# When the mixer tiles run, what lies in the value step, and how the last keys are loaded, in a decode-attention kernel that streams its cache

## The chip, the cores and the metric

The kernel runs on one core of one Trainium2 chip. The metric is the time of one execution in device microseconds. The engines by their names in the profile: PE multiplies matrices (PEld is its weight load), DVE and ACT work on vectors, SP issues the large DMA transfers, POOL does a few instructions at the start. The profile also gives PEclk, the share of its full clock that PE was granted.

## What is computed

One token is decoded: a gated sum of grouped-query attention over a cache of 65,536 positions and a small token-mixing MLP.

```python
Hq, Hkv, Sk, Dh = 16, 8, 65536, 256          # x is 1 x 448
q = (x @ wq), by heads;  k, v: each of the 8 cached heads serves 2 query heads
scores = q @ k.T * Dh**-0.5
a = softmax(scores) @ v, heads side by side, @ wo

h = layernorm(x)
u = gelu(outer(h, w1) + b1)                   # 448 x 1792, tanh form
b = u @ w2 + b2                               # 448

g = sigmoid(sum(x * gate_w))
out = g * a + (1 - g) * b
```

All is bf16. K and V are 268 MB each, so 537 MB of the 544 MB that the kernel reads are cache.

## The kernel before

**Pairs.** For each of the 8 cached heads (H) the 65,536 positions are cut into 4 parts (PPH) of 16,384. A part is called a pair here, a pair of one K load and one V load of 8 MB each; there are NP = 32. A pair's keys are 128 tiles of 128 positions (NV), worked on in 8 chunks (BODY) of 16 tiles. V is held in one buffer of 128 tiles (`vbuf`), K in a ring of one and a half (`kring`, NV + HV tiles, HV = 64): the half of it at HV holds the first four chunks of every pair, and the other four lie in turn at 0 and at NV.

**A pair on PE.** `keys` (L371) transposes chunks 0 to 6 into PSUM (`transposes`, L331, the tile `kst`), and after each but the first multiplies the chunk before by the two queries (`scores`, L356). DVE and ACT bring the transposed banks to SBUF (`evacuate`, L670, into `ktT`, two banks on DVE, two on ACT at L812). Transposing into a bank waits until the chunk before in it was evacuated (L342). `values` (L404) then adds the products of the pair before: 8 matmuls for the denominators (L391), 128 with the V tiles (`some`, L396). `last_keys` (L378) does chunk 7, and `maxima` (L384 on PE, L678 on DVE) finds the running maximum over the partitions. ACT makes the exponentials (`weights`, L793), DVE rescales the accumulator (L695 to L703) and announces it on `s_acc`.

**The loop of PE** (L537 to L580) has NP + LEAD + 1 = 35 passes. Registers say whether a pass does keys (L538), values (L550) or a last chunk (L569); what a pass doesn't do is jumped over. In the first passes values of pair 0 come before keys of pair 1, and so on; from pair 3 on a pass is: keys of pair j, values of pair j - 1, last chunk of pair j, maxima of pair j.

**The code of `values`** holds, in this order: denominators, the first 48 products for the usual pair, the last pair's alternative (four products of the mixer's row with the gate, L419, and 48 products with V tiles that were loaded into `kring`), products 48 to 112, products 112 to 128, and for the last pair the whole tail (`tail`, L475: products by the other operand order, L443, and the last projection, L469). Behind `values`, and ahead of the last chunk, stands the end of a head (L558 to L568): PE clears the accumulator, sums it over the rows (L455) and projects it with wo (L466).

**DVE's loop** (L746 to L762): chunks 0 to 6 evacuated; at the first pair of a new head `finish_head` (L724) for the head before; chunk 7; maxima; in pairs 0 to 13 one tile of the mixer (`mixer`, L643); behind a head's last pair the new queries (`qcur`, L760), which PE's keys wait for (L543). A mixer tile is 11 DVE instructions on 128 x 448 (L649 to L667) and one tanh on ACT (L816); PE multiplies it with w2 one pair later (L574 to L578).

**The order of the loads** (SP, L282 to L306) is written out and waits by semaphores. K of pair j is issued once PE has transposed four chunks of pair j - 1 (L287); V of pair j, once values of pair j - 1 are done (`sem_pv`, L275). For a new head SP then waits for the old head's projection and loads the next wo (L278 to L280). V of the last pair comes in pieces (L301 to L306): 48 tiles into `kring` once pair 30's keys are transposed, the other four pieces once its values are done, then wo in two pieces. All of these go through one queue, in the order of their issue.

K of pair LEAD = 2 and of pair 3 are loaded in halves with semaphores of their own (`sem_kc`, L197, L285 to L292), which PE waits for at chunk 4 (L336 to L338).

Of the kernel before, what the change touches and what calls it, by code (L numbers as in the profile page):

```python
# [7 lines left out]
AF = mybir.ActivationFunctionType  # L8
# [4 lines left out]
def bass_gated_mix__gqa_block_cached__mixer_token_mlp__decode_kernel(  # L13
# [63 lines left out]
    GC0 = 0.796875  # L77
    GC1 = 0.044677734375

    assert FT <= NP - PPH  # L80

# [13 lines left out]
    with ctx:  # L95
# [98 lines left out]

        sem_k = new_sem("sem_k")
        sem_kb = new_sem("sem_kb")
        sem_kc = [new_sem("sem_kc%d" % i) for i in range(2)]  # L197
# [55 lines left out]
        def _(eng):  # L253
# [28 lines left out]
            for j in range(NP):  # L282
                if j == LEAD + 1:
                    eng.wait_ge(sem_tr[NB - 1], BODY * LEAD)
                    load(kring, A_k_cache, j, HV, NV, HV, sem_kc[1])  # L285
                if j >= 1:
                    eng.wait_ge(sem_tr[NB - 1], BODY * (j - 1) + DC)  # L287
                if j == LEAD:
                    load(kring, A_k_cache, j, HV, NV, 0, sem_k)
                    load(kring, A_k_cache, j, 0, HV, 0, sem_kc[0])  # L290
                elif j == LEAD + 1:
                    load(kring, A_k_cache, j, 0, HV, HV, sem_k)  # L292
                elif j >= 1:
# [33 lines left out]
        def _(pe):  # L327
# [3 lines left out]
            def transposes(k, c, j, u16, x2):  # L331
                if k == 0:
                    pe.wait_ge(sem_k, u16)
                if k == DC:
                    pe.wait_ge(sem_kb, 16)
                    for i, sem in enumerate(sem_kc):  # L336
                        with pe.If(j == LEAD + i):
                            pe.wait_ge(sem, 16)  # L338

                def tiles(at):  # L340
                    for b in range(NB):
                        pe.wait_ge(sem_ev[b], c + 1)  # L342
                        for i in range(4):
                            ins = pe.transpose(kst[:, b, i * P:(i + 1) * P],  # L344
                                               kring_f[:, at + NT * (k % DC) + 4 * b + i, :], ident[:, :])
# [56 lines left out]
                return ins  # L402

            def values(v):  # L404
                def last(f):
                    with pe.If(v == NP):
                        f()

                pe.wait_ge(s_acc, v)
                pe.wait_ge(sem_exp, pe.snap(v + 1, min_val=2, max_val=NP + 1))  # L410
                denominators()
                with pe.If(v < NP):
                    pe.wait_ge(sem_v, pe.snap(v * 16, min_val=16, max_val=16 * NP))
                    some(0, NRING, vbuf)
                with pe.Else():
                    pe.wait_ge(s_mix, 1)
                    for q in range(NCG):
                        r = slice(32 * q, 32 * q + 1)
                        pe.matmul(prj[r, 0:WG], rest[r, :], brow[r, :], start=False, stop=True,  # L419
                                  skip_group_check=True)  # L420
                    piece_wait(0)
                    some(0, NRING, kring)
                for n0, n1 in pieces[1:]:
                    if n0 < NLATE:
                        last(lambda: piece_wait(n0))
                        ins = some(n0, n1, vbuf)
                ins.then_inc(s_early, 1)
                with pe.If(v < NP):
                    some(NLATE, NV, vbuf).then_inc(sem_pv, 1)
                with pe.Else():  # L430
                    tail()

            def piece_wait(n):
                for (n0, _), sem in zip(pieces, sem_vp):
# [95 lines left out]
            gk_reg = reg("gk_reg", 1)  # L530
            mv_reg = reg("mv_reg", 0)
            gv_reg = reg("gv_reg", 1)
            def val(r, lo=0, hi=NP):
                return pe.snap(r, min_val=lo, max_val=hi)

            on = OrderedEngineSet([pe.engine])
            with nc.Fori(0, NP + LEAD + 1, 1, engines=on, head_slot={pe.engine: 0}):  # L537
# [12 lines left out]
                with pe.If(val(v_reg) < val(l_reg)):  # L550
# [4 lines left out]
                    values(v)  # L555
                    with pe.If(v >= LEAD):
                        pe.reg_mov(cap_reg, NP)
                    with pe.If(val(mv_reg) == PPH):  # L558
                        with pe.If(v < NP):
                            pe.reg_mov(mv_reg, 0)  # L560
                            g1 = pe.snap(gv_reg, min_val=1, max_val=H)
                            pe.wait_ge(s_cp, g1)
                            clear(acc[:, 0:NACC])
                            by_row(acc[:, SELC:NACC]).then_inc(s_sel, 1)
                            pe.wait_ge(sem_wo, pe.snap(g1 * 16, min_val=16, max_val=16 * H))
                            pe.wait_ge(s_oTn, g1)
                            project(range(2 * REP)).then_inc(s_proj, 1)
                            pe.reg_add(gv_reg, gv_reg, 1)  # L568
                with pe.If(val(l_reg) < val(k_reg)):  # L569
                    l = pe.snap(l_reg, min_val=0, max_val=NP - 1)  # L570
                    last_keys(pe.snap(l * BODY, min_val=0, max_val=NC), pe.snap(x2l_reg, min_val=0, max_val=NV))
                    pe.reg_sub(x2l_reg, NV, x2l_reg)
                    with pe.If(l > 0):
                        with pe.If(l < FT + 1):  # L574
                            pe.wait_ge(s_pb, val(l_reg, 1))
                            for q in range(NCG):
                                pe.matmul(prj[32 * q:32 * q + 1, WG:2 * WG], w2cur[:, :],
                                          gu[:, q * WG:(q + 1) * WG], start=False, stop=True, skip_group_check=True)  # L578
                    pe.reg_add(l_reg, l_reg, 1)
                    maxima(pe.snap(l_reg, min_val=1, max_val=NP))  # L580

        @block.vector
        def _(vec):
# [192 lines left out]
        def _(act):  # L776
# [12 lines left out]

            pt_reg = act.alloc_register("pt_reg")  # L790
            act.reg_mov(pt_reg, DC)

            def weights(j1):  # L793
                act.wait_ge(s_mneg, j1)
# [11 lines left out]
            with nc.Fori(0, NP, 1, engines=OrderedEngineSet([act.engine])) as j:  # L806
# [4 lines left out]
                        act.wait_ge(sem_tr[b], c0 + (k + 1))  # L811
                        act.activation(ktT[:, k % KTB, b, :], kst_b[:, b, :], AF.Copy).then_inc(sem_ev[b], 1)  # L812
                weights(act.snap(j + 1, min_val=1, max_val=NP))
                with act.If(j < FT):
                    act.wait_ge(s_u, j + 1)
                    act.activation(z_b[:, :], z_b[:, :], AF.Tanh).then_inc(s_tanh, 1)  # L816
# [32 lines left out]
```

## Time and profile before

| | us |
|---|---|
| three executions | 1271.89, 1272.1, 1273.35 (median 1272.1) |
| the profiled execution: its own time | 1273.45 |
| its span, first to last instruction | 1271.7 |
| PE busy (matmuls) / weight loads | 941.5 / 884.7 |
| ACT busy / DVE busy | 545.8 / 498.2 |
| DMA: read in all, mean rate | 544.22 MB, 428 GB/s |

The busy times are shares of the whole span (74, 70, 43 and 39%) and say nothing of single stages. The large queue (q1) carried 544.22 MB, and its packets took 99.2% of 16 engines' span. In a timeline a row is: start, duration, engine, line, operation, output <- input, shape, count, and in brackets how long the engine had been idle and what ended that. "issue" there means that the profile shows nothing that the engine waited for. In a windows view a row is: window, its length, then for each engine busy time and count, then granted clock, DMA share and GB/s.

### The profile page before, as it was taken

The numbers are of one execution on the slowest core, as the hardware profiler recorded it, in microseconds if no ns is written. First come the engines' busy times: TensorE is split into PE (matmuls) and PEld (weight loads), VectorE is DVE, ScalarE is ACT, GpSimd is POOL, SyncE is SP. The second block draws the span as 40 slices with busy tenths as digits, with TensorE's granted clock in tenths as the row PEclk, the third lists the DMA queues.
The fourth block names the chain that finished last, engine by engine and source line by source line (L and its number), as shares of the span: only waits on it lengthen the run. The fifth ranks groups of instructions, "written<-read, shape, count | busy, mean of one in ns | idle before, by whom it ended". The sixth has DMA issues, their size and how long they took to land.

```text
span 1271.7 us, 40084 instructions
## 1 busy us (share of the span) xinstructions
PE 941.5 (74%) x17201; PEld 884.7 (70%) x17201; DVE 498.2 (39%) x1125; ACT 545.8 (43%) x692; POOL 0.9 (0%) x7
## 2 busy tenths in 40 slices
PE   4678877787676787766877667786678766698667
PEld 3567767787675786756877567776668766687666
DVE  3335444444543434433434234342333332343333
ACT  2345443454433544434544335453344443344432
POOL 0000000000000000000000000000000000000000
PEclk9889688888878988878977789877798877888778
DMA  9999899999999999999999999999999999999998
GB/s 415 430 399 428 377 429 429 443 429 429 429 429 443 429 429 451 439 410 449 441 429 429 443 429 429 429 443 429 429 429 429 443 429 429 429 451 439 429 429 344
DMA packets 11912, 544.40 MB, mean 428 GB/s; under 512 B 1401, under 2 KB 1660, under 8 KB 2940
## 3 DMA queue, kind: packets, MB, share of 16 engines
q1 hardware_dynamic: 11810, 544.22, 99.2%
q8 instruction: 9, 0.15, 0.0%
q10 hardware_dynamic: 90, 0.01, 0.0%
q14 instruction: 3, 0.02, 0.0%
HBM read 544.22 MB, written 0.00 MB: 428 GB/s over the span
## 4 chain that ended last, share of the span: by engine, by line
DMA 61%; PE 35%; DVE 2%; issue 2%; DVEq 0%; ACT 0%; SPq 0%
DMA kring<-in_A_k_cache_dram 61%; PE kst L344 27%; PE sps L365 6%; PE acc L400 2%; PE sps L388 0%; DVE mcol L680 0%; ACT z_b L816 0%; PE acc L458 0%; PE sps L386 0%; PE acc L393 0%; DVE ktT L674 0%; DVE mrow L685 0%; DVE z_b L655 0%; DVE wtmp L653 0%; DVE z_b L659 0%
## 5 line engine op out<-in xcount | busy, mean ns | idle before, releaser
L344 PE MATMUL kst<-ident,kring 128*128 128x128 f32 x4096 | 574.9, 303 | 251.6 <-DMA kring<-in_A_k_cache_dram 198.0
L812 ACT ACTIVATE ktT<-kst 128x1024 bf16<-128x1024 bf16 x512 | 500.4, 1021 | 560.7 <-PE kst L344 560.0
L344 PEld LDWEIGHTS kst<-ident,kring 128*128 128x128 f32 x4096 | 522.2, 158 | 266.6 <-issue 259.7
L674 DVE COPY ktT<-kst 128x1024 bf16<-128x1024 bf16 x512 | 354.0, 692 | 606.3 <-PE kst L344 582.2
L365 PEld LDWEIGHTS sps<-qcur,ktT 128*128 128x128 bf16 x8192 | 239.4, 97 | 3.0
L365 PE MATMUL sps<-qcur,ktT 128*128 128x2 bf16 x8192 | 237.5, 163 | 0.0
L400 PE MATMUL acc<-vbuf,pT 128*2 128x256 bf16 x4032 | 121.6, 281 | 2.9 <-issue 2.9
L400 PEld LDWEIGHTS acc<-vbuf,pT 128*2 128x2 bf16 x4032 | 94.2, 86 | 21.9 <-issue 3.4
L795 ACT ACTIVATE fade<-mdif 128x2 f32<-128x2 f32 x32 | 6.5, 203 | 93.6 <-DVE mdif L691 93.6
L388 PEld LDWEIGHTS sps<-mdiag,mones 2*128 2x128 f32 x64 | 12.1, 234 | 28.1 <-DVE mdiag L687 28.1
L680 DVE TENSOR_REDUCE mcol<-sps 128x2 f32<-128x256 f32 x32 | 13.6, 425 | 45.7 <-PE sps L365 45.7
L388 PE MATMUL sps<-mdiag,mones 2*128 2x2 f32 x64 | 14.8, 299 | 21.3 <-DVE mdiag L687 21.3
L799 ACT ACTIVATE pT<-sps,mneg 128x64 f32 x128 | 30.3, 334 | 0.0
L816 ACT ACTIVATE z_b<-z_b 128x448 bf16<-128x448 bf16 x14 | 8.1, 576 | 48.1 <-DVE z_b L661 48.1
L386 PE MATMUL sps<-ident,mcol 128*2 128x128 f32 x32 | 9.3, 292 | 18.7 <-DVE mcol L683 18.7
L393 PE MATMUL acc<-pT,ones_sq 128*128 128x32 bf16 x256 | 11.7, 179 | 9.8 <-DVE acc L703 5.2
L708 DVE COPY accs<-acc 128x288 f32<-128x288 f32 x8 | 3.7, 458 | 38.8 <-PE acc L400 38.8
L386 PEld LDWEIGHTS sps<-ident,mcol 128*2 128x2 f32 x32 | 2.6, 80 | 22.1 <-DVE mcol L683 22.1
L393 PEld LDWEIGHTS acc<-pT,ones_sq 128*128 128x128 bf16 x256 | 8.6, 97 | 12.4 <-issue 7.0
L703 DVE TENSOR_SCALAR acc<-acc,fader 128x256 f32<-128x256 f32 x32 | 15.8, 493 | 2.5
L685 DVE TENSOR_REDUCE mrow<-sps 2x1 f32<-2x128 f32 x32 | 8.9, 279 | 12.3 <-PE sps L386 12.3
L690 DVE TENSOR_SCALAR mneg<-sps 128x2 f32<-128x2 f32 x32 | 5.1, 159 | 17.8 <-PE sps L388 17.8
(108 smaller groups left out, 169.4 us busy)
## 6 DMA issues: line engine op xcount, KB each, us to landing
kring<-in_A_k_cache_dram SPq DMA_DIRECT2D x6, 4096.0 KB, 23.6
wo_sb<-in_A_wo_dram SPq DMA_DIRECT2D x7, 448.0 KB, 32.0
vbuf<-in_A_wq_dram SPq DMA_DIRECT2D x1, 3072.0 KB, 10.6
kring<-in_A_v_cache_dram SPq DMA_DIRECT2D x1, 3072.0 KB, 38.3
vbuf<-in_A_v_cache_dram SPq DMA_DIRECT2D x1, 3072.0 KB, 10.1
vbuf<-in_A_v_cache_dram SPq DMA_DIRECT2D x1, 1024.0 KB, 12.2
vbuf<-in_A_v_cache_dram SPq DMA_DIRECT2D x1, 768.0 KB, 13.7
vbuf<-in_A_wq_dram SPq DMA_DIRECT2D x1, 512.0 KB, 11.4
```

What stands on the lines that cost most here:

```text
L344: ins = pe.transpose(kst[:, b, i * P:(i + 1) * P], kring_f[:, at + NT * (k % DC) + 4 * b + i, :], ident[:, :])
L365: ins = pe.matmul(sps[:, 0, 2 * (NT * k + nt):2 * (NT * k + nt) + 2], ktT[:, par, b, ntl * DH + dj:(ntl + 1) * DH:2], qcur[:, dj, :], star ...
L386: pe.transpose(mxT, mcol[:, :], ident[:, :]).then_inc(s_mT, 1)
L388: pe.matmul(mxB, mones[:, :], mdiag[:, :], start=True, stop=True).then_inc(s_mB, 1)
L393: pe.matmul(acc[:, DENC:SELC], ones_sq[:, :], pT[:, r, :], start=False, stop=(r == BODY - 1), skip_group_check=True)
L400: ins = pe.matmul(acc[o:o + REP, 0:DH], pT[:, r, 2 * nt:2 * nt + 2], buf[:, n, :], start=False, stop=False, skip_group_check=True)
L674: vec.tensor_copy(ktT[:, k % KTB, b, :], kst_b[:, b, :]).then_inc(sem_ev[b], 1)
L680: vec.tensor_reduce(out=mcol[:, :], in_=scores_all.rearrange("p (n hh) -> p hh n", hh=REP), axis=AX.X, op=ALU.max)
L685: vec.tensor_reduce(out=mrow[:, :], in_=mxT, axis=AX.X, op=ALU.max)
L703: vec.tensor_scalar(acc[:, 0:DENC], acc[:, 0:DENC], fader[:, :], None, op0=ALU.mult).then_inc(s_acc, 1)
L799: ins = act.activation(pT[:, bass.ds(p0, DC), hh:2 * NT:REP], scores_all.rearrange("p (a r n hh) -> p a hh r n", a=2, r=DC, hh=REP)[:, hal ...
L812: act.activation(ktT[:, k % KTB, b, :], kst_b[:, b, :], AF.Copy).then_inc(sem_ev[b], 1)
```

## The change

Four edits.

1. **Mixer tiles** run in pairs 4 to 17 (MIX0 = LEAD + 2) instead of 0 to 13, on DVE, ACT and PE alike.
2. **The value step** loses its alternatives: `values` now holds the denominators, 128 products and the waits, 136 matmuls with their weight loads. The last pair's first products (mixer's row, 48 products with `kring`) become `first_of_last`, which stands behind `maxima` of the last pair in the loop's body; the tail stands at the end of the loop's body.
3. **The end of a head** moves from behind `values` to behind `last_keys`, ahead of the mixer's product and of `maxima`; on DVE `finish_head` moves behind the evacuation of chunk 7.
4. **K of the last pair** is loaded in two halves of 4 MB, the second with a third semaphore `sem_kc[2]`, which PE waits for at chunk 4.

```diff
+    MIX0 = LEAD + 2
...
+                elif j == NP - 1:
+                    load(kring, A_k_cache, j, 0, HV, HV, sem_k)
+                    load(kring, A_k_cache, j, HV, NV, HV, sem_kc[2])
...
-                    for i, sem in enumerate(sem_kc):
-                        with pe.If(j == LEAD + i):
+                    for p, sem in zip((LEAD, LEAD + 1, NP - 1), sem_kc):
+                        with pe.If(j == p):
                             pe.wait_ge(sem, 16)
...
             def values(v):
...
                 denominators()
                 with pe.If(v < NP):
                     pe.wait_ge(sem_v, pe.snap(v * 16, min_val=16, max_val=16 * NP))
                     some(0, NRING, vbuf)
-                with pe.Else():
-                    pe.wait_ge(s_mix, 1)
-                    for q in range(NCG):
...
-                    piece_wait(0)
-                    some(0, NRING, kring)
                 for n0, n1 in pieces[1:]:
...
                 with pe.If(v < NP):
                     some(NLATE, NV, vbuf).then_inc(sem_pv, 1)
-                with pe.Else():
-                    tail()
+
+            def first_of_last():
+                pe.wait_ge(s_acc, NP)
+                pe.wait_ge(sem_exp, NP + 1)
+                pe.wait_ge(s_mix, 1)
+                for q in range(NCG):
+                    r = slice(32 * q, 32 * q + 1)
+                    pe.matmul(prj[r, 0:WG], rest[r, :], brow[r, :], start=False, stop=True,
+                              skip_group_check=True)
+                piece_wait(0)
+                some(0, NRING, kring)
...
                     values(v)
...
-                    with pe.If(val(mv_reg) == PPH):
-                        with pe.If(v < NP):
-                            pe.reg_mov(mv_reg, 0)
...
                 with pe.If(val(l_reg) < val(k_reg)):
...
                     last_keys(pe.snap(l * BODY, min_val=0, max_val=NC), pe.snap(x2l_reg, min_val=0, max_val=NV))
                     pe.reg_sub(x2l_reg, NV, x2l_reg)
-                    with pe.If(l > 0):
-                        with pe.If(l < FT + 1):
-                            pe.wait_ge(s_pb, val(l_reg, 1))
+                    with pe.If(val(mv_reg) == PPH):
+                        pe.reg_mov(mv_reg, 0)
+                        g1 = pe.snap(gv_reg, min_val=1, max_val=H)
+                        pe.wait_ge(s_cp, g1)
+                        clear(acc[:, 0:NACC])
+                        by_row(acc[:, SELC:NACC]).then_inc(s_sel, 1)
+                        pe.wait_ge(sem_wo, pe.snap(g1 * 16, min_val=16, max_val=16 * H))
+                        pe.wait_ge(s_oTn, g1)
+                        project(range(2 * REP)).then_inc(s_proj, 1)
+                        pe.reg_add(gv_reg, gv_reg, 1)
+                    with pe.If(l > MIX0):
+                        with pe.If(l < MIX0 + FT + 1):
+                            pe.wait_ge(s_pb, val(mix_reg, 1, FT))
+                            pe.reg_add(mix_reg, mix_reg, 1)
...
                     maxima(pe.snap(l_reg, min_val=1, max_val=NP))
+                    with pe.If(val(l_reg) == NP):
+                        first_of_last()
+                with pe.If(val(v_reg) == NP):
+                    tail()
...
-                    for k in range(BODY - 1):
+                    for k in range(BODY):
                         evacuate(k, c0 + k)
                     with vec.If(j > 0):
                         with vec.If(m < 1):
                             finish_head(g)
-                    evacuate(BODY - 1, c0 + (BODY - 1))
                     maxima(vec.snap(j + 1, min_val=1, max_val=NP), c0)
-                    with vec.If(j < FT):
-                        mixer(j)
+                    with vec.If(j >= MIX0):
+                        with vec.If(j < MIX0 + FT):
+                            mixer(vec.snap(kt_reg, min_val=0, max_val=FT - 1))
...
-                with act.If(j < FT):
-                    act.wait_ge(s_u, j + 1)
+                with act.If(j >= MIX0):
+                    with act.If(j < MIX0 + FT):
+                        act.wait_ge(s_u, act.snap(mix_reg, min_val=1, max_val=FT))
```

More of the change, by code (lines that the diff above doesn't have):

```diff
@@ L78, in bass_gated_mix__gqa_block_cached__mixer_token_mlp__decode_kernel @@
     GC1 = 0.044677734375
-    assert FT <= NP - PPH
+    MIX0 = LEAD + 2
+    assert MIX0 + FT <= NP - PPH
     HV = NV // 2
@@ L196, in bass_gated_mix__gqa_block_cached__mixer_token_mlp__decode_kernel @@
         sem_kb = new_sem("sem_kb")
-        sem_kc = [new_sem("sem_kc%d" % i) for i in range(2)]
+        sem_kc = [new_sem("sem_kc%d" % i) for i in range(3)]
         s_qc = new_sem("s_qc")
@@ L404, in values @@
             def values(v):
-                def last(f):
-                    with pe.If(v == NP):
-                        f()
                 pe.wait_ge(s_acc, v)
@@ L414, in values @@
                     some(0, NRING, vbuf)
-                with pe.Else():
-                    pe.wait_ge(s_mix, 1)
-                    for q in range(NCG):
-                        r = slice(32 * q, 32 * q + 1)
-                        pe.matmul(prj[r, 0:WG], rest[r, :], brow[r, :], start=False, stop=True,
-                                  skip_group_check=True)
-                    piece_wait(0)
-                    some(0, NRING, kring)
                 for n0, n1 in pieces[1:]:
                     if n0 < NLATE:
-                        last(lambda: piece_wait(n0))
+                        with pe.If(v == NP):
+                            piece_wait(n0)
                         ins = some(n0, n1, vbuf)
@@ L532, in _ @@
             gv_reg = reg("gv_reg", 1)
+            mix_reg = reg("mix_reg", 1)
             def val(r, lo=0, hi=NP):
@@ L557, in _ @@
                         pe.reg_mov(cap_reg, NP)
-                    with pe.If(val(mv_reg) == PPH):
-                        with pe.If(v < NP):
-                            pe.reg_mov(mv_reg, 0)
[L561 to L568, printed above, removed]
                 with pe.If(val(l_reg) < val(k_reg)):
@@ L791, in _ @@
             act.reg_mov(pt_reg, DC)
+            mix_reg = act.alloc_register("mix_reg")
+            act.reg_mov(mix_reg, 1)
             def weights(j1):
@@ L813, in _ @@
                 weights(act.snap(j + 1, min_val=1, max_val=NP))
-                with act.If(j < FT):
-                    act.wait_ge(s_u, j + 1)
-                    act.activation(z_b[:, :], z_b[:, :], AF.Tanh).then_inc(s_tanh, 1)
+                with act.If(j >= MIX0):
+                    with act.If(j < MIX0 + FT):
+                        act.wait_ge(s_u, act.snap(mix_reg, min_val=1, max_val=FT))
+                        act.activation(z_b[:, :], z_b[:, :], AF.Tanh).then_inc(s_tanh, 1)
+                        act.reg_add(mix_reg, mix_reg, 1)
             act.wait_ge(s_proj, H)
```

## The prediction

> **What bounds the kernel now.** I read the page first, then the table by stage, then the timeline of four places, then the landings of the big loads.
>
> ```profile
> span 1271.7 us, 40084 instructions
> ...
> DMA packets 11912, 544.40 MB, mean 428 GB/s; under 512 B 1401, under 2 KB 1660, under 8 KB 2940
> ```
>
> The transfers fill the span. By the trace's landings a K or V load of 8 MB lands 19.36 us after the one before it (V 429.44, K 448.80, V 468.14), which is the pace of the stream; from K of pair 6 on (253.95) none is more than 0.3 us behind that, wo loads of 1.1 us aside. So time can only come from the places where the stream stops, from before it starts, or from after it ends. There are three. The first is the windows view around 150 us (bytes are booked where a packet starts):
>
> ```profile
> 145.00:150.00 5.00, 5.00 (x75) 4.94 (x72) 1.38 (x2) 2.70 (x3) 0.00 (x0) 0.50 0.97 419
> 150.00:152.00 2.00, 2.00 (x11) 2.00 (x11) 0.69 (x1) 0.32 (x2) 0.00 (x0) 0.50 0.00 0
> 152.00:154.50 2.50, 2.33 (x40) 2.18 (x38) 0.69 (x1) 1.88 (x2) 0.00 (x0) 0.66 0.00 0
> 154.50:157.00 2.50, 2.21 (x33) 2.21 (x34) 1.34 (x2) 1.12 (x3) 0.00 (x0) 1.00 1.26 419
> ```
>
> The last two columns are DMA share and GB/s: for 4.5 us no packet starts, while PE is busy at a granted clock of 0.50. The timeline says what SP was waiting for:
>
> ```profile
> 134.65 3.67 PE L344 MATMUL kst<-ident,kring 128*128 128x128 f32 x16 [0.68 <-issue]
> ...
> 135.74 0.34 DVE L649 TENSOR_SCALAR wtmp<-hbT,params 128x448 bf16<-128x448 bf16 x1 [0.18 <-issue]
> ...
> 139.71 0.39 DVE L667 TENSOR_TENSOR gu<-wtmp,z_b 128x448 bf16<-128x448 bf16 x1
> 140.42 1.29 DVE L674 COPY ktT<-kst 128x1024 bf16<-128x1024 bf16 x2 [0.32 <-issue]
> 141.17 3.67 PE L344 MATMUL kst<-ident,kring 128*128 128x128 f32 x16 [2.85 <-DVE ktT L674]
> ...
> 153.57 0.33 SPq L264 DMA_DIRECT2D kring<-in_A_k_cache_dram  x1
> ```
>
> Pair 3's first chunk is transposed at 134.65, but DVE evacuates it only after pair 2's mixer tile (L649 to L667), so the second chunk waits 2.85 us. Four chunks must be transposed before K of pair 4 is issued, and that is at 153.57; V of pair 2 had landed at 152.09, its last packets started at 149.3. K of pair 4 lands 23.25 us after it: **3.89 us lost** (23.25 - 19.36).
>
> The second place is earlier. V of pair 1 lands at 93.65, K before it at 72.46: 21.19, so **1.83 us lost**. Its issue waits for the first value step:
>
> ```profile
> 51.43 3.54 PE L344 MATMUL kst<-ident,kring 128*128 128x128 f32 x16 [8.06 <-issue]
> ...
> 60.87 4.32 PE L400 MATMUL acc<-vbuf,pT 128*2 128x256 bf16 x80
> ...
> 68.09 2.52 PE L400 MATMUL acc<-vbuf,pT 128*2 128x256 bf16 x48 [2.90 <-issue]
> ...
> 70.64 0.33 SPq L264 DMA_DIRECT2D vbuf<-in_A_v_cache_dram  x1
> 74.70 5.59 PE L344 MATMUL kst<-ident,kring 128*128 128x128 f32 x32 [4.09 <-issue]
> ```
>
> "issue" gaps of 8.06, 2.90 and 4.09 us occur in the first passes only; over the rest of the loop the longest is 0.7 (waits view, 250 to 1215). The page's queue row counts 9 instruction packets on q8, and all 9 start before 78 us (at 43.4, 48.3, 65.6 and 70.4 just inside these gaps). So these are code that PE reaches for the first time: the jump over the value step (8.06, two packets), the step's product 80 (2.90), the jump over the head's end.
>
> The third place is the tail: after V of pair 30 lands (1247.04), PE still has a value step, the last chunk, maxima, exponentials and the last products.
>
> ```profile
> 1248.31 3.66 PE L400 MATMUL acc<-vbuf,pT 128*2 128x256 bf16 x128
> 1252.02 1.86 SPq L264 DMA_DIRECT2D vbuf<-in_A_v_cache_dram  x4
> ...
> 1260.99 2.73 PE L400 MATMUL acc<-kring,pT 128*2 128x256 bf16 x48
> 1263.51 3.35 PE L400 MATMUL acc<-vbuf,pT 128*2 128x256 bf16 x64
> ```
>
> Here stream and PE end together: the last wo piece lands at 1268.60, PE's last late product ends at 1268.86.
>
> **The change, part by part.**
>
> *Mixer in pairs 4 to 17.* Fourteen tiles of 4.4 us (135.74 to 140.10) on DVE are moved, none removed. Pairs 0 and 1 had them hidden: K of pair 1 lands at 72.46, the tile of pair 0 ends at 65.0; pair 1's ends at 106.9, DVE is next needed at 110.36. Pair 2's goes: DVE is free at 135.55, PE runs chunks 0 and 1 back to back, 134.65 to 142 at the half clock. In every later pair where PE ran 32 transposes in one go the clock rose 2.9 to 5.5 us after their start (254.08 to 259.5, 331.69 to 334.59); in pair 3 the split run stayed at half until 153.68. With the clock up by 137.6 to 141, chunk 3 ends at 144.8 to 147 and K is issued then; it takes 0.96 us to its first packet (153.57 to 154.53) and the stream has room until 149. So the whole 3.89 goes, with 1 to 3 us to spare. In pairs 4 to 17 the tile lies beside the wait for K: PE waited 184.9 us in 25 pairs (7.4 each) with tiles in a third of them, and every pair from 253.95 on starts within 0.2 us of its K. Tightest is pair 4, with a head's end: values at about 190, last chunk, head's end, maxima, tile to about 211, K of pair 5 at about 208; K of pair 6 goes out near 220.5, room until 224.4. Cost 0; uncovered, it would be at most what pair 3 shows.
>
> *Value step of 272 instructions.* The jump skips 136 products and their weight loads (272), not 263 (526): the two ring variants, the tail and the head's end lie behind it now. At least one packet of the 8.06 gap should go (about 3.5 us by the 2.9 and 4.09 gaps), and the step is short enough that no code in it is skipped whole before its first run, so the 2.90 should go too. Bounds: 0 gained if packets fall on other boundaries, 1.83 if V of pair 1 is issued before about 68.5. I take 1.8: it needs 2.1 us of some 6. The stream then reaches K of pair 3 1.8 us sooner (118.64, at most 1 us of room); pair 1's keys start at 72.6 in place of 74.70 without the 2.24 us after K's landing, so that issue moves up 2.1 as well.
>
> *Head's end behind the last chunk.* 25 products, DVE's finish and SP's wait before the wo load (up to 2.8 us now, some 4 more then; next on SP is a K load 20 us later). DVE's finish stands behind eight evacuations; queued behind it are the maxima, needed by the next value step 25 us on. Cost 0, covered by the same 7.4 us per pair.
>
> *Last K load in two halves, first products behind the last maximum.* One DMA more (0.4 us of issue, queue full: 0). The first half lands 9.7 us sooner, at 1217.7; PE begins pair 31 at about 1220.6 (maxima end 1219.8) instead of 1227.82, chunk 4 at 1232 finds the second half (1227.7), and keys end at about 1240.5 (20 us as now). But the value step needs V of pair 30, 1247.04, and PE then stands idle for 6 us. It starts 1 us sooner than now (1248.02), but at the half clock: 54 ns a product (4.32/80 above) until one full clock step of 3.41 us was busy, against 28.6 (3.66/128). That is 5.2 to 6.8 us, so it ends at 1252.4 to 1254.0, not 1251.97: **+0.4 to +2.0, I take +1.2**, and the four V issues at 1252.02 move with it, as do last chunk, maxima and exponentials. Then the loop's return (1.6 us in the timeline at 107.97, mostly run ahead of the 2.7 us of products) and the 0.4 us of denominators, which now lie under the wait for the mixer's row, come between the 48 products and the 64: +0.4 to +1.5; a clock already up would give back 1. Together the end comes **1.6 us later** against the stream (from -0.5, if the clock holds, to +2.8).
>
> The Trainium skill, "TensorE: Matmul & The Clock Gate", under "What's actually happening", has the array fall to half after an idle window of about 3.4 us and rise after a busy one. The trace's clock records agree (only 0.5 and 1.0, steps of 3.41 us). By that rule the split load costs the tail; without it the sum would be 1 us better.
>
> Sum: -3.89 - 1.83 + 1.6 = -4.1 us. The profiled execution took 1273.45 (span 1271.7 and 1.75 around it), so 1269.3 after. The runs' median is 1272.1, 1.35 below. If those runs lost less at 150 us (the half clock there ends by a chance of phase), 1269.3 stands; if they are shorter otherwise, 1268.0. I take the middle: **1268.7**, -0.27%.
>
> **Rivals.**
> 1. *The tail costs nothing or gains* (the clock holds through the idle 6 us, or PE's head start carries): -5.7 - 0.5 gives 1267.3 to 1265.9. For it: V's four issues come after a gap of 0.5 us in the stream that could close. Against: every idle stretch of 5 us in the trace shows 0.5. 0.17.
> 2. *A stall comes back*: pair 1's fetches stay, because the step is no shorter for the machine than it was (1.83 not gained), or pair 5 breaks up as pair 3 did, 18.9 us from first transpose to issue, 2.9 us lost. 1268.7 + 1.8 to 2.9 gives 1270.5 to 1271.6. Against: the room worked out above. 0.20.
> 3. *Slower: code at the end is fetched late.* First products and tail run once, behind the loop's body. If their code isn't in PE's store when reached, each jump costs what L550's did, 3.5 to 7.6 us; it decides once both are missed: 1268.7 + 7.6 gives 1276.3. Against: the tail ran for the first time at 1261 to 1269 before, without an issue gap or a q8 packet. 0.05. The Trainium skill, "Runtime: NRT & Kernel Launch", "Instruction fetch mechanics", says that a taken branch out of a two-page window forces a fetch; by that, misses would recur in every pass, and no q8 packet after 78 us bears it out here.
>
> The forecast (1267.3 to 1270.5) has 0.58. A measurement here tells about 0.2%, 2.5 us: faster needs under 1269.6. Forecast mostly (0.48 of 0.58) and rival 1 fall there: 0.65; same 0.29; slower 0.06. The range takes in rival 1's middle and rival 2: 1266.3 to 1272.2.
>
> **What would show it.** Right: no window near 150 without packets, K of pair 4 landing 19.4 after V of pair 2; gaps of 8.06 and 2.90 smaller, V of pair 1 landing 19.4 after K; pair 31's value step at clock 0.50 and longer than 5 us; 48 and 64 products apart. Wrong: a packetless window elsewhere, an issue gap at the end, or the value step of pair 31 at full clock.

## The result, and the profile after

The changed kernel takes 1269.23 us (median of 15 executions, 1267.54 to 1270.73), the kernel before 1273.85 (15 executions beside them, 1269.61 to 1274.74). The ratio is 0.9968 [0.996, 0.9976]: **faster by 0.32%**. The profiled execution of the changed kernel took 1268.60 with a span of 1266.8; the one of before took 1273.45.

The page of the changed kernel:

```profile
span 1266.8 us, 40261 instructions
...
DMA packets 12054, 544.37 MB, mean 430 GB/s; under 512 B 1417, under 2 KB 1676, under 8 KB 2956
...
q8 instruction: 7, 0.11, 0.0%
```

The same bytes at 430 GB/s in place of 428; q8 had 9 packets before.

The windows view of the changed kernel around 150 us (columns: window, length, busy time of PE, PEld, DVE, ACT and POOL with counts, PEclk, DMA share, GB/s):

```profile
143.00:147.00 4.00, 3.33 (x55) 3.24 (x54) 1.87 (x4) 2.44 (x3) 0.00 (x0) 1.00 0.76 328
147.00:149.00 2.00, 2.00 (x45) 1.99 (x44) 0.91 (x2) 1.44 (x2) 0.00 (x0) 1.00 1.22 524
149.00:151.50 2.50, 2.50 (x49) 2.49 (x48) 1.30 (x3) 1.94 (x2) 0.00 (x0) 1.00 0.97 419
151.50:154.00 2.50, 2.35 (x65) 2.19 (x66) 1.12 (x2) 1.94 (x2) 0.00 (x0) 1.00 0.97 419
```

The clock is 1.00 where it was 0.50, and the stretch without packets is gone. The timeline of the changed kernel has the reason:

```profile
132.65 6.05 PE L348 MATMUL kst<-ident,kring 128*128 128x128 f32 x32 [1.42 <-issue]
...
139.34 1.94 PE L348 MATMUL kst<-ident,kring 128*128 128x128 f32 x16
...
143.90 0.33 SPq L265 DMA_DIRECT2D kring<-in_A_k_cache_dram  x1
```

Pair 3's chunks 0 and 1 run as one stretch of 32 transposes, the clock rises in it (the chunk at 139.34 takes 1.94 us in place of 3.67), and K of pair 4 is issued at 143.90 in place of 153.57. K of pair 4 lands 19.33 us after V of pair 2.

The second place, in the timeline of the changed kernel:

```profile
53.60 3.67 PE L348 MATMUL kst<-ident,kring 128*128 128x128 f32 x16 [9.51 <-issue]
...
61.26 0.37 PE L390 MATMUL sps<-ident,mcol 128*2 128x128 f32 x1 [2.30 <-issue]
...
64.92 5.74 PE L404 MATMUL acc<-vbuf,pT 128*2 128x256 bf16 x128
70.71 0.33 SPq L265 DMA_DIRECT2D vbuf<-in_A_v_cache_dram  x1
72.56 3.83 PE L348 MATMUL kst<-ident,kring 128*128 128x128 f32 x32 [1.90 <-DMA kring<-in_A_k_cache_dram]
```

The gap inside the value step (2.90) is gone: its 128 products are one row. But the last chunk of pair 0 starts at 53.60 and not at 51.43, and a new gap of 2.30 stands ahead of its maxima. V of pair 1 is issued at 70.71; before it was 70.64.

The tail in the timeline of the changed kernel:

```profile
1241.79 6.09 PE L404 MATMUL acc<-vbuf,pT 128*2 128x256 bf16 x128 [5.61 <-DMA vbuf<-in_A_v_cache_dram]
1247.94 1.85 SPq L265 DMA_DIRECT2D vbuf<-in_A_v_cache_dram  x4
...
1256.46 2.73 PE L404 MATMUL acc<-kring,pT 128*2 128x256 bf16 x48
...
1259.79 2.23 PE L404 MATMUL acc<-vbuf,pT 128*2 128x256 bf16 x64 [0.27 <-issue]
```

PE waits 5.61 us for V of pair 30, then the value step runs at the half clock (6.09 against 3.66 before) and 48 and 64 products stand apart, as was forecast. What was not: the 64 products take 2.23 us, not 3.35, since the clock is up by 1260.5.

Where the 4.85 us between the two profiled executions lie, by landings of the big loads. A load lands on 16 engines; "last" is what a consumer waits for:

| | before, first / last | after, first / last |
|---|---|---|
| K of pair 1 | 70.47 / 72.46 | 70.40 / 72.42 |
| V of pair 1 | 91.88 / 93.65 | 91.90 / 92.67 |
| V of pair 2 | 150.33 / 152.09 | 150.24 / 150.95 |
| K of pair 4 | 174.80 / 175.34 | 169.60 / 170.28 |
| V of pair 30, last | 1247.04 | 1241.75 |
| output issued, after V of pair 30 | +23.08 | +23.53 |

By last landings: about 1 us at V of pair 1, 3.93 at K of pair 4, and 0.45 given back in the tail. By first landings everything comes from K of pair 4: the microsecond at V of pair 1 is only that the engines that were latest are less late (spread 0.77 against 1.76 us).

### The profile page after: what moved, and what is told of

Same layout as the page of the kernel before. It is cut to its first block, busy times and chain, and to the rows that moved or that the text cites. A ratio compares the mean times of both kernels' runs of the same rounds, so it can differ in the third digit from the quotient of the medians.

```text
span 1266.8 us, 40261 instructions
## 1 busy us (share of the span) xinstructions
PE 922.7 (73%) x17201; PEld 867.2 (68%) x17201; DVE 497.1 (39%) x1125; ACT 544.0 (43%) x692; POOL 0.9 (0%) x7
## 4 chain that ended last, share of the span: by engine, by line
DMA 68%; PE 30%; issue 1%; DVE 0%; SPq 0%; DVEq 0%
DMA kring<-in_A_k_cache_dram 65%; PE kst L348 24%; PE sps L369 5%; DMA vbuf<-in_A_v_cache_dram 3%; PE acc L404 2%; PE acc L397 0%; PE sps L392 0%; DVE mcol L687 0%; PE sps L445 0%; PE sps L452 0%; DVE acc L710 0%; PE sps L390 0%; DVE mrow L692 0%; DVE accs L715 0%; DVE mdiag L694 0%
## 5 line engine op out<-in xcount | busy, mean ns | idle before, releaser
L348 PE MATMUL kst<-ident,kring 128*128 128x128 f32 x4096 | 555.5, 296 | 266.8 <-DMA kring<-in_A_k_cache_dram 233.5
L348 PEld LDWEIGHTS kst<-ident,kring 128*128 128x128 f32 x4096 | 504.7, 154 | 281.3 <-issue 280.6
L460 PEld LDWEIGHTS acc<-sel,accs 128*64 128x64 f32 x112 | 10.8, 214 | 0.9
```

The source lines that it names most:

```text
L348: ins = pe.transpose(kst[:, b, i * P:(i + 1) * P], kring_f[:, at + NT * (k % DC) + 4 * b + i, :], ident[:, :])
L460: ins = pe.matmul(dst[hh * HP:(hh + 1) * HP, i:i + 1], accs[:, i:DH:2 * REP], sel[:, hh:hh + 1], start=False, stop=True, skip_group_check= ...
```

## The experiments

Times are medians, each with its ratio to the kernel before run beside it on the same chip; those of before were 1273.22, 1273.43 and 1273.02 in the three groups below.

### First group: the parts of the change one at a time

**mix_only**: the kernel before, with the mixer's tiles moved and nothing else.

```diff
+    MIX0 = LEAD + 2
...
-                    with vec.If(j < FT):
-                        mixer(j)
+                    with vec.If(j >= MIX0):
+                        with vec.If(j < MIX0 + FT):
+                            mixer(vec.snap(kt_reg, min_val=0, max_val=FT - 1))
...
```

> The kernel before, with the mixer tiles moved to pairs 4 to 17 and nothing else. Theory M (the tile of pair 2 held up pair 3's second chunk, and with it the issue of K of pair 4): the whole stall near 150 us goes, K of pair 4 lands 19.4 us after V of pair 2 instead of 23 to 24.5, and with no split load at the end the time is that of before less 5.1: about 1268.7, if before is at 1273.85. Rival C (the gain came from the shorter value step and the moved head's end, by which PE was 2 us earlier in the first pairs): the stall stays at over half its size, time 1271.5 or more.

Measured: 1268.92, 0.9971 [0.9959, 0.9984]. As far as the times can tell, this part alone brings what the whole change brings. Its timeline of pair 3:

```profile
135.18 6.24 PE L345 MATMUL kst<-ident,kring 128*128 128x128 f32 x32 [0.72 <-issue]
...
144.65 1.95 PE L345 MATMUL kst<-ident,kring 128*128 128x128 f32 x16
```

Chunks 0 and 1 are one stretch again, K of pair 4 is issued at 146.62 and lands 19.35 us after V of pair 2: the whole stop is gone.

**no_mix**: the changed kernel with the tiles back in pairs 0 to 13.

```diff
-    MIX0 = LEAD + 2
+    MIX0 = 0
```

> The changed kernel, with the mixer tiles back in pairs 0 to 13. Theory M: the stall near 150 us is back; pair 3 begins 2 us sooner than in the kernel before (132.7, not 134.65), so K of pair 4 is issued near 151 and 2 to 4 us are lost: 1271.3 to 1273.3, where the changed kernel has 1269.2. Rival C: within 0.8 us of the changed kernel.

Measured: 1269.38, 0.9975 [0.9964, 0.9987]. The median is not where the theory of the tile wanted it. But the twelve executions are two groups, seven at 1267.57 to 1269.47 and five at 1271.12 to 1272.98, and the profiled one (1272.98) is of the upper. Its timeline:

```profile
133.90 3.67 PE L348 MATMUL kst<-ident,kring 128*128 128x128 f32 x16 [1.43 <-DMA kring<-in_A_k_cache_dram]
139.69 3.68 PE L348 MATMUL kst<-ident,kring 128*128 128x128 f32 x16 [2.12 <-DVE ktT L681]
...
152.09 0.33 SPq L265 DMA_DIRECT2D kring<-in_A_k_cache_dram  x1
```

The tile delays DVE, PE waits 2.12, the chunks run at the half clock, and K of pair 4 lands 21.74 us after V of pair 2: 2.4 lost. The lower group suggests that this does not happen in every execution; no_mix_again below shows it.

**whole_key**: the changed kernel with the last K load in one piece.

```diff
-                elif j == NP - 1:
-                    load(kring, A_k_cache, j, 0, HV, HV, sem_k)
-                    load(kring, A_k_cache, j, HV, NV, HV, sem_kc[2])
...
-                    for p, sem in zip((LEAD, LEAD + 1, NP - 1), sem_kc):
+                    for p, sem in zip((LEAD, LEAD + 1), sem_kc):
```

> The changed kernel, with the last K load in one piece again. Theory T (the split load makes PE idle for 5.6 us ahead of pair 31's value step, which then runs at the half clock): PE starts pair 31 some 6 us later, the value step runs at full clock (3.7 us, not 6.1), V's last four loads are issued 1 to 1.3 us sooner after V of pair 30 has landed, and the end is 0.3 to 1.2 us sooner: about 1268.5. Rival H (the head start on pair 31 is worth its 1 us): 0.5 to 1 us slower than the changed kernel, 1270.

Measured: 1269.11, 0.9968 [0.9956, 0.9979], the same as with the split. Its timeline at the end:

```profile
1244.67 3.67 PE L401 MATMUL acc<-vbuf,pT 128*2 128x256 bf16 x128
1248.38 1.85 SPq L265 DMA_DIRECT2D vbuf<-in_A_v_cache_dram  x4
...
1260.51 3.15 PE L401 MATMUL acc<-vbuf,pT 128*2 128x256 bf16 x64 [0.27 <-issue]
```

The value step is at full clock as the theory said, V is issued 5.34 us after V of pair 30 landed (6.19 with the split). But now the 64 products fall into the half clock (3.15 against 2.23), and the output goes out 23.89 after that landing (23.53 with the split). What is won in front is lost behind.

**split_only**: the kernel before, with the last K load in two halves and nothing else.

```diff
+                elif j == NP - 1:
+                    load(kring, A_k_cache, j, 0, HV, HV, sem_k)
+                    load(kring, A_k_cache, j, HV, NV, HV, sem_kc[2])
...
```

> The kernel before, with the last K load in two halves and nothing else. Theory T: the value step of pair 31 takes 5.2 to 6.8 us instead of 3.7 and V's last four loads go out 0.4 to 2 us later against V of pair 30; the end comes 0.4 to 2 us later: about 1274.9 if before is at 1273.85. Rival H: 0.5 to 1 us sooner, 1273.

Measured: 1273.87, 1.0006 [0.9994, 1.0018]. In its trace the value step takes 6.30 at the half clock and the output goes out 0.7 us later against V of pair 30 than before: the direction that was expected, too small for the times to tell.

### Second group: which tile, and what else could be won

**one_tile**: the kernel before, with only pair 2's tile left out of its place (tiles in pairs 0, 1 and 3 to 14).

```diff
-                    with vec.If(j < FT):
-                        mixer(j)
+                    with vec.If(j < FT + 1):
+                        with vec.If(j != LEAD):
+                            mixer(vec.snap(kt_reg, min_val=0, max_val=FT - 1))
...
```

> The kernel before, with the mixer tiles in pairs 0, 1 and 3 to 14: only pair 2 is left without one. Theory M (pair 2's tile alone): the time of the kernel in which all of them moved, 1268.9 within 0.8. Rival N (the tile of pair 3, behind which the new queries of pair 4 wait, costs as well): 1270.5 or more.

Measured: 1269.46, 0.9964 [0.995, 0.9978]; K of pair 4 is issued at 146.80 and lands 19.35 us after V of pair 2. One tile of fourteen is the whole of it, as far as the times can tell.

**clock_up**: the kernel before, tiles where they were, with 24 more transposes behind pair 2's maxima that only keep PE busy while it would wait for DVE. They write to `prj`, the bank in which the mixer's sums stand, and the output is changed, so this kernel serves for its time and trace alone.

```diff
+                    with pe.If(val(l_reg) == LEAD + 1):
+                        for _ in range(24):
+                            pe.transpose(prj[:, 2 * P:3 * P], ident[:, :], ident[:, :])
```

> The kernel before, with 24 transposes of the identity (into columns of prj that nothing reads) put on PE behind pair 2's maxima: work added, the mixer's tile of pair 2 and DVE's delay left as they are. Theory K (the delay of 2.85 us matters because it splits the run of 32 transposes, so that the clock stays at 0.50 for all four chunks, 4.35 us each instead of 2.6): PE is busy without a break from about 134 on, the clock is up by 140, K of pair 4 is issued near 148 instead of 153.6, and 3 to 5 us are gained: 1268.5 to 1270.5, where before has 1273.2. Rival D (the delay itself is what costs): no gain, 1273 or more.

Measured: 1277.69, 1.0035 [1.0021, 1.0049], slower. In the trace the suspected mechanism does what it should: pair 3 runs at full clock, and K of pair 4 lands 20.07 us after V of pair 2 (0.7 lost, not 3.9). The time goes elsewhere: 11 instruction packets on q8 in place of 9, K of pair 2 issued at 94.43 (85.49 before), and the first halves late with it.

**fill**: the changed kernel, with 1 MB of pair 2's keys issued ahead of V of pair 1, to fill the gap that is left there.

```diff
+                    eng.wait_ge(sem_tr[NB - 1], BODY)
+                    load(kring, A_k_cache, LEAD, 0, NT, 0, sem_kc[0])
...
-                    load(kring, A_k_cache, j, 0, HV, 0, sem_kc[0])
+                    load(kring, A_k_cache, j, NT, HV, 0, sem_kc[0])
```

> The changed kernel, with 1 MB of pair 2's keys (16 tiles, for chunk 4, whose place in the ring is free once pair 0's keys are transposed) issued ahead of V of pair 1. Theory F (the stream still stops for 2 us between K and V of pair 1, because V's issue waits for the first value step at 70.7): the gap is filled, V of pair 1 lands within 0.5 us of now, all behind it 1.5 to 2.1 us sooner, and K of pair 4 is still issued in time: 1267.3. Rival P (PE's first pairs are the bound, and the stop moves to K of pair 3 or 4): within 0.7 us of the changed kernel, 1269.2.

Measured: 1268.69, 0.9959 [0.9946, 0.9973]: 4.74 us under the kernel before, where the changed kernel is 4.62 under its own. A gain of 1.9 is not there, and one of a few tenths can't be told from none. The gap is filled (first landings 70.69, 73.15, 92.78: the pace of the stream), and two things take the gain back. By first landings the keys of pair 2 are 1.56 us sooner than in the changed kernel (109.80 against 111.36), but K of pair 4, issued at 146.79 in place of 143.90, only 0.62 (168.98 against 169.60): part of rival P. And the last landings stay 1.8 to 2.5 us behind the first, so that V of pair 30 lands in full at 1242.18, against 1241.75.

**tail**: the changed kernel, with the last chunk ahead of the values in every pass, and 64 tiles of the last V in `kring`.

```diff
-    NRING = 48
+    NRING = 64
...
+                with pe.If(val(l_reg) < val(k_reg)):
+                    l = pe.snap(l_reg, min_val=0, max_val=NP - 1)
+                    last_keys(pe.snap(l * BODY, min_val=0, max_val=NC), pe.snap(x2l_reg, min_val=0, max_val=NV))
+                    pe.reg_sub(x2l_reg, NV, x2l_reg)
                 with pe.If(val(v_reg) < val(l_reg)):
...
-                    last_keys(pe.snap(l * BODY, min_val=0, max_val=NC), pe.snap(x2l_reg, min_val=0, max_val=NV))
-                    pe.reg_sub(x2l_reg, NV, x2l_reg)
```

> The changed kernel, with the last chunk ahead of the value step in every pass (so that in pair 31 it fills the idle time before V of pair 30) and the first V piece of the last pair at 64 tiles instead of 48. Theory E (at the end the stream runs dry for 1.5 us before V's last four pieces, which wait for pair 31's value step, and PE then needs last chunk, maxima and exponentials): no gap in the stream behind the piece in kring, exponentials 3 us sooner, the end 1.5 to 2.5 us sooner: 1267.2. Rival S (V's loads, now issued 3.6 us later in every pair, or the wait for the last piece take it back): 1269 or more.

Measured: 1272.22, 0.9991 [0.9982, 1.0]. The tail is what was wanted (output issued 21.79 after V of pair 30, 1.7 better), but the first passes lose more than that. Its timeline there:

```profile
64.58 0.58 PE L392 MATMUL sps<-mdiag,mones 2*128 2x2 f32 x2 [0.66 <-DVE mdiag L696]
71.99 0.40 PE L397 MATMUL acc<-pT,ones_sq 128*128 128x32 bf16 x8 [6.83 <-issue]
...
78.23 0.33 SPq L265 DMA_DIRECT2D vbuf<-in_A_v_cache_dram  x1
```

A gap of 6.83 us at the loop's return, and V of pair 1 issued at 78.23.

### Third group: the two mechanisms again, with less code

**clock_up2**: clock_up with 9 wide matmuls, fewer instructions, into a bank that is free.

```diff
+                    with pe.If(val(l_reg) == LEAD + 1):
+                        pe.wait_ge(sem_ev[0], BODY * (LEAD + 1) + 1)
+                        for _ in range(9):
+                            pe.matmul(kst[:, 0, 0:DM], ones_sq[:, :], hbT[:, :], start=True, stop=True)
```

> The kernel before, with nine more matmuls on PE behind pair 2's maxima (into PSUM that the next transposes overwrite), so short that the loop's code doesn't grow over the next code page, as it did with the 24 transposes (those also cleared the mixer's first sums). The mixer's tile of pair 2 stays. Theory K (clock): pair 3's later chunks take 2.6 us each, K of pair 4 is issued 13.5 to 16.5 us after the last matmul of pair 2's maxima, not 19.6, and the time is 3 to 5 us under before: 1268.5 to 1270.5. Rival D (the delay on DVE): 1273 or more.

Measured: 1277.4, 1.0039 [1.0025, 1.0052], slower. Its timeline around pair 3:

```profile
139.86 3.54 PE L584 MATMUL kst<-hbT,ones_sq 128*128 128x448 bf16 x9
...
147.13 1.97 PE L344 MATMUL kst<-ident,kring 128*128 128x128 f32 x16 [0.81 <-DVE ktT L678]
...
154.30 0.33 SPq L264 DMA_DIRECT2D kring<-in_A_k_cache_dram  x1
```

With the tile still ahead of it, PE runs its chunks at 1.97 us, K of pair 4 is issued 14.4 us after the first extra matmul (before: 18.9 after the first transpose) and lands 20.01 after V of pair 2. Both the stream and PE come to this place later than before, V of pair 2 by 4.0 and PE by 5.2 us, so PE had no more room than before. So the trace bears the mechanism out, and the time again does not: 11 instruction packets, K of pair 2 issued at 91.75, and pair 5's chunks broken up.

**tail_out**: tail, with the last pair's products and the tail taken out of the loop's body (34 passes).

```diff
-            with nc.Fori(0, NP + LEAD + 1, 1, engines=on, head_slot={pe.engine: 0}):
+            with nc.Fori(0, NP + LEAD, 1, engines=on, head_slot={pe.engine: 0}):
...
-                    with pe.If(val(l_reg) == NP):
-                        first_of_last()
-                with pe.If(val(v_reg) == NP):
-                    tail()
+            first_of_last()
+            denominators()
...
+            tail()
```

> The kernel with the last chunk ahead of the value step and a first piece of 64 tiles, with the last pair's products and the tail put behind the loop (34 passes). Theory P (that kernel gained 1.7 us behind V of pair 30, and lost 5.8 us between K and V of pair 1 only because four more instructions put the loop's last branch on another code page): V of pair 1 is issued near 70.5 again, not 78.2, and the end stays 1.7 us nearer to V of pair 30: 1267.3. Rival L (the order itself makes the first passes late): V of pair 1 still issued at 75 or later, 1271 or more.

Measured: 1268.09, 0.9964 [0.995, 0.9977]. With less code in the loop V of pair 1 is issued at 70.96 again, and the 4 us that tail lost are back. At the end 1.1 of tail's 1.7 us are left (output issued 22.45 after V of pair 30). In time it is 4.93 us under the kernel before, the changed kernel 4.62; these two can't be told apart.

**tail_out_fill**: tail_out and fill together.

> The same, with 1 MB of pair 2's keys ahead of V of pair 1. If both gains add (0.5 and 1.7 us as measured apart): 1266.7 to 1267.0. If the slowest of the sixteen landings is what counts and keeps its lag: as the kernel without the fill, 1267.3.

Measured: 1267.15 (1266.25 to 1267.98), 0.9957 [0.9944, 0.9971], the lowest median of all, 5.87 us under the kernel before, where the changed kernel is 4.62 under its own: some 1.3 us more, though the intervals of the two ratios overlap. Here the filled gap is kept: K of pair 4 lands 1.51 us sooner than in tail_out (169.54 against 171.05). Its timeline at the end:

```profile
1240.94 3.66 PE L409 MATMUL acc<-vbuf,pT 128*2 128x256 bf16 x128 [0.77 <-DMA vbuf<-in_A_v_cache_dram]
1244.64 1.75 SPq L265 DMA_DIRECT2D vbuf<-in_A_v_cache_dram  x4
```

The last chunk now stands in the 5.61 us in which the changed kernel's PE idles, so the clock holds through the value step, and V is issued 3.75 us after the landing (6.19).

**no_mix_again**: the same kernel as no_mix, executed once more.

> The changed kernel with the tiles back in pairs 0 to 13, once more, for a second profile. Its runs fell in two groups, 1267.6 to 1269.5 and 1271 to 1273, and the profile was of the second. Theory W (where the clock's steps of 3.41 us fall decides): a profile near 1268 shows the clock rising before 148 in pair 3, with the tile of pair 2 still ahead of it; one near 1272 shows 0.50 until 150 or later.

Measured: 1267.57, an execution of the lower group. Its timeline at the place where no_mix lost 2.4 us:

```profile
131.96 3.67 PE L348 MATMUL kst<-ident,kring 128*128 128x128 f32 x16 [1.43 <-issue]
137.75 1.97 PE L348 MATMUL kst<-ident,kring 128*128 128x128 f32 x16 [2.12 <-DVE ktT L681]
...
144.91 0.33 SPq L265 DMA_DIRECT2D kring<-in_A_k_cache_dram  x1
```

The same wait of 2.12 us behind the same tile, and the same first chunk at 3.67. But the clock is up from the second chunk on: K of pair 4 is issued 12.95 us after the first transpose, not 18.2, and lands 19.49 after V of pair 2. So in this execution the tile's delay itself costs next to nothing; it costs where the clock stays at half behind it, which differs between executions of one kernel. Of the 5.4 us between these two executions this explains 2.25; 2.3 more are V of pair 1 (issued 69.84 against 72.47: the last chunk of pair 0 has its code at 53.89 against 55.78, and in the upper one a gap of 2.58 follows), and 0.9 come later.

## Why the prediction was right, and where it was not

**The stop near 150 us (-3.89): right in size and cause.** Measured -3.93 at K of pair 4. mix_only and one_tile bring all of it, and one_tile says which tile. The way it goes is also as written: 32 transposes in one stretch, the clock up, K issued within the room. The two executions of no_mix add what the prediction had only as a remark: the half clock is the price, and DVE's delay only its occasion. One reading was a little off: in the pairs of before the clock rose 2.7 to 6.1 us after the start of 32 transposes, not 2.9 to 5.5; the 141 that it calculated with covers that (134.65 + 6.1). The remark has a consequence for the gain, too. Of the 67 executions of before (15 beside the changed kernel, 52 beside the experiments), 6 lie at 1269.61 to 1270.06 and the others at 1271.72 and more. It may be that in these 6 the clock came up in time; no trace of one was kept, so this is not shown.

**The tiles in pairs 4 to 17 cost nothing: right.** By the landings, no K or V load of the changed kernel up to V of pair 30 lands late; the same stretch from K of pair 4 on took 1071.70 us before and 1071.47 after.

**The shorter value step (-1.83): the step that failed.** The prediction had V of pair 1 issued some 2 us sooner, for one or two instruction packets less in the 8.06 gap. There are two less, 7 for 9, and the gap in the value step is gone, yet V of pair 1 is issued at 70.71 for 70.64. The trace shows where the sum was wrong. Before, the packets on q8 start at 36.4, 43.4, 48.3, 55.6, 65.6, 70.4 and 77.3, after two early ones; in the changed kernel at 36.4, 43.7, 50.7, 58.3 and 65.4. From 43.7 on they come about 7 us apart there, while the data queue is full. The shorter jump did not remove a packet from in front of the last chunk: two start in that gap as before, the second 2.4 us later, and PE goes on 2.9 us after it (53.60). So the chunk waits 9.51 us from the keys on. The 2.90 inside the value step is gone, but a gap of 2.30 stands behind the next packet (58.26), ahead of the maxima; 0.7 of it is DVE's work on the chunk (to 59.66), the rest code. The bound "0 gained if packets fall on other boundaries" was in the text; I took 1.8. By last landings 0.94 was gained, by first landings nothing.

This does not hang on one execution, by which V's issue moves a good deal (69.84 and 72.47 in the two of no_mix): in the seven traces with the shorter step, tail aside, it is issued at 69.84 to 72.47, in the six with the longer one at 69.71 to 73.26. What did come as forecast is the start of pair 1's keys, 72.56 (72.6 forecast) in place of 74.70. K of pair 2, which waits for these keys, goes out sooner with it (81.59 for 85.49), and by first landings that won the stream nothing (101.66 for 101.60).

The Trainium skill, "Runtime: NRT & Kernel Launch", "Instruction fetch mechanics", calls crossing a block of code mostly hidden. From the second pass on nothing here speaks against it (no q8 packet after 66 us); in the first pass the gaps with such packets in front of them, 9.51 and 2.30 us, are not hidden. Why the packets come 7 us apart is open.

**The tail (+1.6): direction right, size +0.45.** The value step at half clock cost 1.21 (V issued +6.19 against +4.98), as forecast. Mis-sized were the terms behind it: the clock came up for the 64 products and gave 1.1 back, which the prediction had only as its lower bound, and the end was set by PE's chain and not by the later V. whole_key shows the trade from the other side. The split load is worth nothing measurable either way: 1269.11 without it, 1269.23 with it, and 1.0006 [0.9994, 1.0018] alone.

**The basis.** I took the middle between the profiled execution and the median of three. Over 15 executions before's median is 1273.85, so the profiled one (1273.45) was typical and its sum, 1269.3, hits the 1269.23. Two errors of about 1 us, one in each direction, cancelled in that sum: 1.83 expected and 0.94 found, 1.6 expected and 0.45 found.

**The gains do not add up, and need not.** The medians of mix_only, one_tile, no_mix and the changed kernel are 1268.92, 1269.46, 1269.38 and 1269.23. The first two take the stop away by the tile. In no_mix the tile stays, and the median is that of a mixture: seven executions in the lower group, five in the upper. Once the stop is gone there is no second one to win.

**The rivals.** The first, a tail that costs nothing, came close in the tail itself (+0.45). The second's half, fetches that stay, is what happened; its other half, pair 5 broken up, was seen in clock_up and clock_up2 (K of pair 6 landing 1.5 to 1.7 us late). The third, code late at the end, was not seen: no q8 packet after 66 us and no issue gap above 0.3 us in the tail. With the tail behind the loop one packet does come late (at 1260.44 in tail_out, 1259.20 in tail_out_fill), but no issue gap follows it on PE.

## What to carry to other kernels

In a kernel bound by its transfers, look for the windows in which no packet starts, and follow each to the one issue that waits; of fourteen moved tiles only the one in front of that issue showed in the time. Ask of a delay not only how long it is but what it does to the PE clock behind it, and run a kernel several times before trusting one phase. In the first passes of a loop, where code is met for the first time under a full queue, count code pages: here it weighed more where the packets fell than how many instructions were saved.

## What the runs showed of the hardware that was not expected

**A few instructions more in a loop can move an issue by 6 to 9 us.** In clock_up (48 more PE instructions), clock_up2 (18 and a wait) and tail (only reordered, with other pieces) PE stands for 10.33, 10.44 and 6.83 us at the loop's return, with packets on q8 in the gap (the last at 79.75, 77.74 and 71.06): K of pair 2 was issued 8.9 and 6.3 us later, and V of pair 1 7.5 us later. tail_out, with the same order and less code in the loop, does not have it. That the return had been pushed onto a page of code that was not yet there is how I read this; no run moves the page alone.

**The engines of one load land apart and stay so.** First and last of 16 landings are 0.3 to 3 us apart (0.68 for K of pair 4 in the changed kernel, 2.97 in one_tile), and the difference is carried for as long as the stream runs; a stop takes it away (1.76 to 0.54 at before's stop near 150 us). So closing a gap also keeps the lag that the gap would have cleared: by first landings the stop cost 5.1 us, by last ones 3.9. What makes engines lag is open.

**Half clock through a busy stretch.** PE is busy for all of 143 to 154 us in before and stays at 0.50 to 0.56; over the whole stretch from 134.65 to 153.68 it is busy for 16.18 of 19.03 us. The Trainium skill, "TensorE: Matmul & The Clock Gate", "What's actually happening", has the clock rise after about 3.4 us of sustained work, counted in windows that run freely. The free phase agrees with no_mix and no_mix_again (the clock fell at 131.73 and rose at 152.21 in one, 129.40 and 136.23 in the other); that a mix of 128x2 scores and transposes counts as too little work would explain the 19 us at half clock, but no run here counts activity.
